# Attention followed by a mixture of experts on one core: how expert weights are loaded, and the last expert's second layer

## The chip, the core and the metric

The kernel runs on one core of a Trainium2 chip, as one program. The time is that of the whole program on the device, in microseconds (us). The core has five engines with a queue each: TensorE (PE, matrix products into the accumulator memory PSUM), VectorE (DVE), ScalarE (ACT), GpSimd (POOL) and SyncE (SP). Here SP issues most of the transfers (DMA), POOL the indirect ones, ACT a few. Each queue is worked off in order, so an instruction that waits holds up everything behind it.

## The reference

```
scores = (q @ k^T) / sqrt(64);  scores = cap * tanh(scores / cap)     # 8 batches x 12 heads, 448 x 448
attn   = softmax(scores);  x = attn @ v, as 3584 tokens x 768
probs  = softmax(x @ w_gate)           # 8 experts; each token goes to its argmax, gate = that probability
for each expert e: the (at most capacity = 80) tokens with the largest gates
    out[token] = gate * (relu(x[token] @ w1[e]) @ w2[e])              # w1: 768 x 1024, w2: 1024 x 768
all other rows of out are zero
```

All data are fp32.

## The kernel before

The attention runs in 24 units (3 of each batch), one per turn of a loop over `w` (line 1488). A turn works through a list of steps (STEPS, at the end LAST, lines 1470 to 1472): `q` score products, `e` exponentials, `v` and `r` products with the values, `x` the place where rows of the PE array change banks (`swap`, line 1221), `l` transfers, `b` background work. The turn `w == NU` has no scores left; its `q` steps begin the first expert (`begin`, line 1450).

Tokens of the first five batches are ranked early, so four experts can be chosen and their tokens fetched before the attention ends. The expert part then runs 84 jobs in a fixed order (line 819): a0, a1, b0, a2, b1, a3, b2, b3, a4, a5, b4, b5, where a is an expert's first layer (6 chunks of weights, 512 KB each) and b its second (8 chunks, 384 KB each). `chunk` (line 859) multiplies one chunk with the tokens in three groups `g` of 32 and four column blocks `j`. After a second layer, `put` (line 892) weights the result with the gates, 12 copies of 32x192 from PSUM to `ys`, and POOL scatters `ys` to the output.

Weights come through a ring of buffers in the order of the jobs: 8 buffers of their own (`wpre`) and 10 (`w3`, line 1545) that lie where the attention's tiles were, 18 in all. `more(n)` (line 826) issues loads on SP until n have been issued. It is called in each turn's transfers (line 1485), for the 8 own buffers, and then once per job (line 1604), always 18 chunks ahead. A load waits until its buffer is free. The transfers on SP and ACT share eight completion counters in turn (DMAHW0 to DMAHW7); a transfer also waits for the one that used its counter before.

The rows of `x` (tile `xb`) of a batch are written to DRAM by four transfers on SP (`write`, line 1277), and the gates of those tokens (tile `gr`) by one more (`send`, line 342), for the last batch on ACT's queue. After both, POOL gathers the tokens of experts 4 and 5 from there (`fetch`, line 1572), ACT and POOL cut them into pieces (`xq`), and DVE turns them into `xt`.

For the last expert (vi = 5, tiles `hp5a`, `hp5b`, `yp5a`, `yp5b`), the second layer's result lies in two PSUM banks: groups 0 and 1 in `yp5a`, group 2 in `yp5b`, and its 12 copies are divided between ACT (even j) and DVE (odd j). `compare` and `decide` (lines 908, 937) set a flag that all engines read at the end (line 1639).

## Time and profile before

| | |
|---|---|
| median of 3 runs | 455.82 us (454.74 to 456.12) |
| the profiled execution | 456.44 us |
| its span on the core | 454.67 us |
| granted TensorE clock, mean | 0.987 of full speed |
| busy share PE, DVE, ACT, POOL | 95%, 51%, 73%, 54% |
| bytes moved | 101.22 MB, 223 GB/s over the span |

The profile is of the one profiled execution. A page gives busy time of each engine and the chain of waits that ended last; the same trace answers for any stretch what an engine did, what ended the idle time before an instruction (in square brackets) and how full the 16 DMA engines were. PE instructions overlap, so the time of a merged row divided by its count is the pace, and PE ends are modelled. The attention fills about the first 345 us, the experts the rest.

### The profile page before, as it was taken

What the parts mean: (1) busy time and instruction counts of PE and PEld (TensorE: products, weight loads), DVE (VectorE), ACT (ScalarE), POOL (GpSimd) and SP (SyncE); (2) the same over time, 40 slices, a digit from 0 to 9 for tenths busy, and PEclk for the clock granted to TensorE, in tenths of its full rate; (3) what the DMA queues carried; (4) which work ended last, traced back from release to release, by engine and by line L of the source; (5) the groups of instructions that cost most, each with busy time, mean ns of one, the idle gap of its engine ahead of it and who ended that gap; (6) DMA issues with size and microseconds to landing.
All of it is one profiled execution on the core that took longest, in us unless ns stands there. A gap on an engine that the chain in (4) does not pass through costs nothing.

```text
span 454.7 us, 21513 instructions
## 1 busy us (share of the span) xinstructions
PE 432.4 (95%) x9533; PEld 230.3 (51%) x9533; DVE 233.8 (51%) x756; ACT 331.4 (73%) x386; POOL 246.4 (54%) x277
## 2 busy tenths in 40 slices
PE   7899999999999999999999999999899999989990
PEld 4344544654444444445444544544346766677680
DVE  1033345337534563776259897977855886210002
ACT  5999989989998988897889988879601154257142
POOL 1767766767765675765576766857655110331000
PEclk9899999999999999999999999999999999999996
DMA  6667695697769559863834862874839997999961
GB/s 158 176 176 203 198 268 160 180 288 211 204 179 269 155 162 276 234 187 99 229 88 133 219 176 82 245 207 147 241 107 360 409 414 275 308 368 410 411 253 38
DMA packets 70549, 101.22 MB, mean 223 GB/s; under 512 B 15264, under 2 KB 52896, under 8 KB 70448
## 3 DMA queue, kind: packets, MB, share of 16 engines
q1 hardware_dynamic: 69072, 96.31, 67.9%
q0 software_dynamic: 752, 3.26, 2.3%
q8 instruction: 77, 1.26, 1.2%
q10 hardware_dynamic: 624, 0.18, 0.2%
q14 instruction: 24, 0.20, 0.1%
HBM read 76.13 MB, written 23.90 MB: 220 GB/s over the span
## 4 chain that ended last, share of the span: by engine, by line
PE 75%; DVE 10%; DMA 7%; ACT 3%; issue 2%; POOL 1%; SPq 1%; POOLq 0%; DVEq 0%; ACTq 0%
PE av L1213 22%; PE sc L1179 22%; PE hp L865 6%; PE yp L865 5%; PE sp L1213 4%; PE av L1246 3%; PE sc L1171 3%; DMA w<-in_w_dram 2%; PE sp L1244 2%; PE lgp L1292 2%; DVE gb L515 2%; DMA xge<-xs,gi 1%; PE pd L447 1%; PE hp5a L865 1%; DMA vr<-in_v_dram 1%
## 5 line engine op out<-in xcount | busy, mean ns | idle before, releaser
L1180 ACT ACTIVATE e<-sc 128x896 f32<-128x896 f32 x168 | 150.9, 913 | 31.1 <-PE sc L1179 28.8
L1213 PE MATMUL av<-e,vr 64*32 64x448 f32 x2304 | 164.5, 538 | 2.0 <-DMA vr<-in_v_dram 1.2
L1179 PE MATMUL sc<-qt,kt 64*32 64x448 f32 x2304 | 143.6, 544 | 3.1 <-ACT e L1180 2.7
L1191 POOL TENSOR_TENSOR t<-e 128x448 f32<-128x448 f32 x92 | 104.7, 1159 | 75.1 <-ACT e L1184 75.1
L1184 ACT ACTIVATE e<-e 128x1792 f32<-128x1792 f32 (+1 forms) x96 | 144.7, 1507 | 0.8
L1194 POOL TENSOR_TENSOR t<-t,e 128x448 f32<-128x448 f32 x92 | 104.5, 1158 | 31.9 <-ACT e L1184 31.9
L1213 PEld LDWEIGHTS av<-e,vr 64*32 64x32 f32 x2304 | 54.4, 107 | 61.6 <-issue 40.6
L1179 PEld LDWEIGHTS sc<-qt,kt 64*32 64x32 f32 x2304 | 42.2, 106 | 47.3 <-issue 32.3
L1254 DVE STREAM_TRANSPOSE st<-sp 128x448 f32<-128x448 f32 x24 | 15.6, 650 | 68.4 <-PE sp L1213 65.2
L1246 PE MATMUL av<-e,vr 64*32 64x224 f32 x384 | 46.6, 349 | 0.0
L1213 PE MATMUL sp<-t,ones 64*32 64x448 f32 x368 | 45.2, 536 | 0.0
L901 POOL DMA_INDIRECT out_dram<-ysv,si x6 | 6.7, 1111 | 69.2 <-ACT ysv L900 62.6
L865 PE MATMUL hp<-w,xt 128*32 128x256 f32 x720 | 41.7, 380 | 1.1 <-DVE xt L693 1.1
L865 PE MATMUL yp<-w,thv 128*32 128x192 f32 x960 | 40.8, 326 | 1.7 <-DMA w<-in_w_dram 1.7
L1246 PE MATMUL av<-e,vx 64*32 64x224 f32 x384 | 42.1, 349 | 0.0
L900 ACT ACTIVATE ysv<-yp,gq 32x192 f32<-32x192 f32 x60 | 24.8, 413 | 16.3 <-PE yp L865 7.9
L865 PEld LDWEIGHTS yp<-w,thv 128*32 128x32 f32 x960 | 32.0, 110 | 9.1 <-issue 2.5
L1266 DVE TENSOR_TENSOR x<-av,r 128x448 f32<-128x448 f32 x48 | 27.7, 618 | 14.4 <-PE av L1213 14.4
L865 PEld LDWEIGHTS hp<-w,xt 128*32 128x32 f32 x720 | 23.5, 110 | 16.3 <-issue 2.3
L1246 PEld LDWEIGHTS av<-e,vr 64*32 64x32 f32 x384 | 22.4, 107 | 16.6 <-issue 15.7
L441 DVE TENSOR_SCALAR_CACHE_REDUCE gb<-krow,kc 112x896 bf16<-112x896 f32 (+7 forms) x36 | 29.8, 871 | 0.6 <-PE pd L447 0.6
L1244 PE MATMUL sp<-e,ones 64*32 64x224 f32 x384 | 28.4, 349 | 0.0
(254 smaller groups left out, 443.0 us busy)
## 6 DMA issues: line engine op xcount, KB each, us to landing
w<-in_w_dram SPq DMA_DIRECT2D x36, 512.0 KB, 8.5
w<-in_w_dram SPq DMA_DIRECT2D x48, 384.0 KB, 8.1
vr<-in_v_dram SPq DMA_DIRECT2D x24, 512.0 KB, 3.9
out_dram<-zero SPq DMA_DIRECT2D x14, 768.0 KB, 5.4
xs<-xb SPq DMA_DIRECT2D x32, 336.0 KB, 6.2
kt<-in_k_dram SPq DMA_DIRECT2D x46, 224.0 KB, 5.4
qt<-in_q_dram SPq DMA_DIRECT2D x46, 224.0 KB, 5.3
vx<-in_v_dram SPq DMA_DIRECT2D x48, 32.0 KB, 3.7
```

The costliest lines, as they stand in the source:

```text
L441: nc.vector.tensor_scalar(g, krow[:, x:y], kp, 0.0, op0=ALU.is_ge, op1=ALU.add, accum_out=a)
L865: nc.tensor.matmul(spot(ps, g, q)[32 * j:32 * j + 32], of(g), w[:, q * j:q * j + q], start=(kk == 0 and g % 2 == 0), stop=(kk == last and ...
L900: nc.scalar.activation(dst, src, AF.Copy, scale=gate(g))
L1179: nc.tensor.matmul(ps[32 * m:32 * m + 32, h, :S], st["k", u][w, pr, y:y + 32], st["q", u][w, pr], start=True, stop=True)
L1180: nc.scalar.activation(st["e", u][:, 2 * x:2 * x + 2], ps[:, :, :S], AF.Tanh, scale=st["regs"][0])
L1184: nc.scalar.activation(e, e, AF.Exp, scale=st["regs"][1])
L1191: nc.gpsimd.tensor_tensor(t1[:, h], e[:, h], e[:, 2 + h], op=ALU.add)
L1194: nc.gpsimd.tensor_tensor(st["es", u, pr][:, h], st["es", u, pr][:, h], e[:, 4 + h], op=ALU.add)
L1213: behind(nc.tensor.matmul(ps[32 * g:32 * g + 32, :S], v_, e, start=first, stop=final))
L1244: behind(nc.tensor.matmul(st["sp", u][32 * g:32 * g + 32, HQ * i:HQ * i + HQ], ones[w, 0:32], e, start=(part == 0), stop=False))
L1246: behind(nc.tensor.matmul(st["av", u, f][32 * g:32 * g + 32, HQ * i:HQ * i + HQ], last_of(u, pr, h, i)[w, 32 * f:32 * f + 32], e, start=Fa ...
L1266: nc.vector.tensor_tensor(st["x", u][:, f], st["av", u, f][:, :S], st["r", u], op=ALU.mult)
```

## The change

- The ring has 21 buffers: 9 of their own, 6 at the low end of the memory that the attention leaves and 6 at its high end, as pools of one buffer each, used in the order 5, 4, 3 of the high ones, the six low ones, 0, 1, 2 of the high ones.
- In each turn's transfers `more` may go one step of its formula further, up to 9.
- In the last turn the marker of `swap` is put on ACT's queue, before on SP's.
- The row writes and the gates' writes are declared independent of each other (`apart_from`).
- In `compare` a memset goes from POOL to DVE.
- The last expert's second layer gets four banks: group 0 in `yp5a`, group 1 in `yp5b`, group 2 in `yp5c` (j = 0, 1) and `yp5d` (j = 2, 3). Its first five chunks run as before, its last three (TAIL) group by group: the three chunks of group 0, then its copies, and so on. DVE copies `yp5a` and `yp5c`, ACT `yp5b` and `yp5d`.

```diff
@@ -45,8 +45,11 @@
 CAPMIN = 1.0e-6
 KD = DM // 128
 KF = F // 128
-WPRE = 8
-WMORE = 10
+WPRE = 9
+WLOW = 6
+WHIGH = (5, 4, 3, None, 0, 1, 2)
+WMORE = WLOW + 6
+TAIL = 3
 DIRECT = (23,)
 PLACE = (2650, 1500, 1500, 1880, 2250, 1880)
 SUMS = (1500, 6200)
@@ -331,6 +334,12 @@
                 nc.vector.tensor_tensor(ohvb, rev[:C].rearrange("p (a e) -> p a e", a=1).broadcast_to(sh), up(cm), op=ALU.is_equal)
         return logits_of, choice, key, lambda: gate_weights(sm, sh, tau if ps is None else None, rd, w2, b, gdst, queue)
 
+    def apart_from(own, others, w):
+
+        for o in st[others]:
+            tc.declare_no_dep(w.ins, o.ins, reason="rows and gates lie apart")
+        st[own].append(w)
+
     def gate_weights(sm, sh, tau, rd, w2, b, gdst, queue):
         if tau is not None:
             nc.vector.scalar_tensor_tensor(w2, tau, 1.0, rd, op0=ALU.subtract, op1=ALU.mult)
@@ -339,7 +348,8 @@
         nc.vector.tensor_scalar(g, g, -1.0, 1e-9, op0=ALU.mult, op1=ALU.add, accum_out=dump[:C])
         g8 = sm.tile([C, NC, PITCH - DM], F32, name=f"gr{b}", tag="gr")
         nc.vector.reciprocal(g8, g.rearrange("p (c a) -> p c a", a=1).broadcast_to([C, NC, PITCH - DM]))
-        send = lambda: queue.dma_start(gdst, g8)
+        def send():
+            apart_from("gates_out", "rows", queue.dma_start(gdst, g8))
         if st.get("gates") is None:
             send()
         else:
@@ -852,18 +862,22 @@
         j, b = divmod(kk, 2)
         return lambda g: x[:, 2 * g + b, 32 * j:32 * j + 32]
 
-    def spot(ps, g, n):
-
-        return ps[g // 2][:, QF * (g % 2):QF * (g % 2) + n] if isinstance(ps, tuple) else ps[:, g // 2, QF * (g % 2):QF * (g % 2) + n]
-
-    def chunk(ps, x, w, kk, last, n):
+    def spot(ps, g, n, j):
+
+        w = slice(32 * j, 32 * j + 32)
+        if isinstance(ps, list):
+            return ps[g + (g == NG - 1 and j >= 2)][w, 0:n]
+        return ps[g // 2][w, QF * (g % 2):QF * (g % 2) + n] if isinstance(ps, tuple) else ps[w, g // 2, QF * (g % 2):QF * (g % 2) + n]
+
+    def chunk(ps, x, w, kk, last, n, groups=range(NG)):
 
         q = n // 4
         of = (rows_of if n == F else turned_rows)(x, kk)
-        for g in range(NG):
+        own = isinstance(ps, list)
+        for g in groups:
             for j in range(4):
-                nc.tensor.matmul(spot(ps, g, q)[32 * j:32 * j + 32], of(g), w[:, q * j:q * j + q],
-                                 start=(kk == 0 and g % 2 == 0), stop=(kk == last and g > 0))
+                nc.tensor.matmul(spot(ps, g, q, j), of(g), w[:, q * j:q * j + q],
+                                 start=(kk == 0 and (own or g % 2 == 0)), stop=(kk == last and (own or g > 0)))
 
     def product(ps, x, ws, n):
         for kk, w in enumerate(ws):
@@ -889,15 +903,19 @@
         nc.scalar.copy(th, hv)
         return th
 
-    def put(fp, yp, gate, si, tag, last=False, others=None):
-        ys = fp.tile([SL, DM], F32, name=f"ys{tag}", tag="ys", bufs=2)
-        for g in range(NG):
-            for j in range(4):
-                dst, src = ys[32 * g:32 * g + 32, QD * j:QD * j + QD], spot(yp, g, QD)[32 * j:32 * j + 32]
-                if last and j % 2:
-                    nc.vector.tensor_scalar(dst, src, gate(g), None, op0=ALU.mult)
-                else:
-                    nc.scalar.activation(dst, src, AF.Copy, scale=gate(g))
+    def weighted(ys, yp, gate, g):
+        for j in range(4):
+            dst, src = ys[32 * g:32 * g + 32, QD * j:QD * j + QD], spot(yp, g, QD, j)
+            if isinstance(yp, list) and (g == 0 or g == NG - 1 and j < 2):
+                nc.vector.tensor_scalar(dst, src, gate(g), None, op0=ALU.mult)
+            else:
+                nc.scalar.activation(dst, src, AF.Copy, scale=gate(g))
+
+    def put(fp, yp, gate, si, tag, ys=None, others=None):
+        if ys is None:
+            ys = fp.tile([SL, DM], F32, name=f"ys{tag}", tag="ys", bufs=2)
+            for g in range(NG):
+                weighted(ys, yp, gate, g)
         w = nc.gpsimd.indirect_dma_start(out=out, out_offset=bass.IndirectOffsetOnAxis(ap=si, axis=0),
                                          in_=ys, in_offset=None, bounds_check=T - 1, oob_is_err=False)
         if others is not None:
@@ -910,7 +928,7 @@
         d = sm.tile([32, NPRE, 3], F32, name="cd", tag="cd")
         nc.vector.tensor_tensor(d, tk, tks, op=ALU.not_equal)
         m = sm.tile([32, 32], F32, name="cm32", tag="cm32")
-        nc.gpsimd.memset(m, 0.0)
+        nc.vector.memset(m, 0.0)
         nc.vector.tensor_reduce(m[:, 0:1], d, axis=AX.XY, op=ALU.max)
         mt = sm.tile([32, 32], F32, name="cmt", tag="cmt")
         nc.vector.transpose(mt, m)
...
@@ -1218,9 +1236,9 @@
                 tc.add_manual_dep(mm.ins, st.pop("turned").ins.name, SYNC, reason="rows of the array change banks")
             st["mm"] = mm
 
-        def swap():
-
-            st["turned"] = nc.sync.nop()
+        def swap(eng):
+
+            st["turned"] = eng.nop()
             tc.add_manual_dep(st["turned"].ins, st["mm"].ins.name, SYNC, reason="rows of the array change banks")
         SYNC = mybir.DependencyInfo(mybir.DependencyClass.Sync, mybir.DependencyReason.DATA)
 
@@ -1276,8 +1294,7 @@
             if j == NP - 1:
                 def write():
                     for i in range(4):
-                        nc.sync.dma_start(xsr[b, i],
-                                          st["xt", b][32 * i:32 * i + 32])
+                        apart_from("rows", "gates_out", nc.sync.dma_start(xsr[b, i], st["xt", b][32 * i:32 * i + 32]))
                 if b == B - 1:
                     write()
                 else:
@@ -1482,7 +1499,7 @@
             while st["gates"]:
                 st["gates"].pop(0)()
             if st.get("ordered"):
-                more(min(WPRE, 3 * (w - NU + 6) // 2 - 1))
+                more(min(WPRE, 3 * (w - NU + 7) // 2 - 1))
 
         st["gates"] = []
         for w in range(NU + 1):
@@ -1516,7 +1533,7 @@
                 elif k_ == 't':
                     total_of(w - 1)
                 elif k_ == 'x' and w:
-                    swap()
+                    swap(nc.scalar if w == NU else nc.sync)
                 elif k_ == 'l':
                     transfers(w)
                 elif k_ == 's' and w:
@@ -1542,14 +1559,15 @@
     st["banks"].append("sp")
     gate(B - 1)
     ft = ExitStack()
-    w3 = ft.enter_context(tc.tile_pool(name="w3", bufs=WMORE, reuse_waits="tile"))
+    wlow = [ft.enter_context(tc.tile_pool(name=f"wl{i}", bufs=1, reuse_waits="tile")) for i in range(WLOW)]
     fr = ft.enter_context(tc.tile_pool(name="fr", bufs=1, reuse_waits="tile"))
     fp = ft.enter_context(tc.tile_pool(name="fp", bufs=2, reuse_waits="tile"))
+    whigh = [ft.enter_context(tc.tile_pool(name=f"wh{i}", bufs=1, reuse_waits="tile")) for i in range(WMORE - WLOW)]
     hs0 = relu(fp, st["hp"], "v0")
     a2s.close()
     pfh = ft.enter_context(tc.tile_pool(name="pfh", bufs=1, space=PSUM))
     pft = ft.enter_context(tc.tile_pool(name="pft", bufs=2, space=PSUM, side="right"))
-    wring.order += [w3] * WMORE
+    wring.order += [p for i in WHIGH for p in (wlow if i is None else [whigh[i]])]
     bg.append((550, lambda: turned(last_u, 0), 1))
     bg.append((550, lambda: turned(last_u, 1), 0))
     xv, fin = {}, {}
@@ -1620,13 +1638,22 @@
         else:
             if kk == 0:
                 yp[vi] = (pft.tile([128, 2, 512], F32, name=f"yp{vi}", tag="ht") if vi < NV - 1 else
-                          (pft.tile([128, 512], F32, name=f"yp{vi}a", tag="ht"), pfh.tile([128, 512], F32, name=f"yp{vi}b", tag="hp")))
+                          [misc(f"yp{vi}a"), misc(f"yp{vi}b"), pft.tile([128, 512], F32, name=f"yp{vi}c", tag="ht"),
+                           pfh.tile([128, 512], F32, name=f"yp{vi}d", tag="hp")])
                 if vi < NPRE:
                     st["there"]("gates")
                 gt[vi] = gate_at(gq, vi) if vi < NPRE else gate_at(gq2, vi - NPRE)
-            chunk(yp[vi], ht[vi], wts[i], kk, KF - 1, DM)
+            ys = None
+            if vi < NV - 1 or kk < KF - TAIL:
+                chunk(yp[vi], ht[vi], wts[i], kk, KF - 1, DM)
+            elif kk == KF - 1:
+                ys = fp.tile([SL, DM], F32, name=f"ysv{vi}", tag="ys", bufs=2)
+                for g in range(NG):
+                    for back in range(TAIL - 1, -1, -1):
+                        chunk(yp[vi], ht[vi], wts[i - back], kk - back, KF - 1, DM, (g,))
+                    weighted(ys, yp[vi], gt[vi], g)
             if kk == KF - 1:
-                put(fp, yp[vi], gt[vi], si0[:, vi:vi + 1] if vi < NPRE else fin["si"][0:SL, vi - NPRE:vi - NPRE + 1], f"v{vi}", vi == NV - 1, stored)
+                put(fp, yp[vi], gt[vi], si0[:, vi:vi + 1] if vi < NPRE else fin["si"][0:SL, vi - NPRE:vi - NPRE + 1], f"v{vi}", ys, stored)
         nxt = next((j for j in jobs[i:] if j[0] == "b" and j[2] == 0 and j[1] not in ht), None)
         if nxt is not None and kk == 1 and jobs.index(nxt) - i in (KD - 1, KF - 1):
             ht[nxt[1]] = turn(fp, pft, hs[nxt[1]], f"v{nxt[1]}")```

Below stands what the change moves at three places. Rows are instructions in queue order: line, operation, output and inputs, shape, and in brackets the engines and transfer counters it waits for.

SP's queue where the last batch's rows are written, before. `w_8` and `w_9` are second-layer chunks of expert b2 (`w_6` is its first), `xb` the rows.

```order
L842 DMA w_8_6598<-in_w_dram 128x768 [waits DMAHW6_49,PE_49]
L1279 DMA xs<-xb_5547 32x14x192 [waits DMAHW7_49,DVE_49]
L1279 DMA xs<-xb_5547 32x14x192 [waits DMAHW0_49]
L1279 DMA xs<-xb_5547 32x14x192 [waits DMAHW1_49]
L1279 DMA xs<-xb_5547 32x14x192 [waits DMAHW2_49]
L842 ISA
L842 DMA w_9_6619<-in_w_dram 128x768 [waits DMAHW3_49,PE_49]
```

The same place after. The gates' transfer on ACT's queue (`xs<-gr`) has the counter DMAHW1 before and DMAHW5 after.

```order
L852 DMA w_10_6619<-in_w_dram 128x768 [waits DMAHW0_49,PE_49]
L852 ISA
L852 DMA w_11_6637<-in_w_dram 128x768 [waits DMAHW1_49,PE_49]
L1297 DMA xs<-xb_5549 32x14x192 [waits DMAHW2_49,DVE_49]
L1297 DMA xs<-xb_5549 32x14x192 [waits DMAHW3_49]
L1297 DMA xs<-xb_5549 32x14x192 [waits DMAHW4_49]
L1297 DMA xs<-xb_5549 32x14x192 [waits DMAHW5_49]
L852 ISA
L852 DMA w_12_6658<-in_w_dram 128x768 [waits DMAHW6_49,PE_49]
```

Three more chunks (`w_9` to `w_11`) now stand ahead of the four row writes, and it is the fourth of them, no longer the third, that waits for the counter of the gates.

PE at the end of the last expert's second layer, before: `w_11` to `w_13` are its last chunks, `yp5a` and `yp5b` the banks.

```order
L865 MATMUL yp5a<-w_11_7425,thv_7508 32x192 [waits DMAHW1_49]
L865 MATMUL yp5a<-w_11_7425,thv_7508 32x192 x7
L865 MATMUL yp5b<-w_11_7425,thv_7508 32x192 x4
L865 MATMUL yp5a<-w_12_7439,thv_7508 32x192 [waits DMAHW2_49]
L865 MATMUL yp5a<-w_12_7439,thv_7508 32x192 x7
L865 MATMUL yp5b<-w_12_7439,thv_7508 32x192 x4
L865 MATMUL yp5a<-w_13_7453,thv_7508 32x192 [waits DMAHW3_49]
L865 MATMUL yp5a<-w_13_7453,thv_7508 32x192 x7
L865 MATMUL yp5b<-w_13_7453,thv_7508 32x192 x4
```

The same chunks after:

```order
L879 MATMUL yp5a<-w_11_7409,thv_7541 32x192 x3
L879 MATMUL yp5a<-w_12_7425,thv_7541 32x192 [waits DMAHW2_49]
L879 MATMUL yp5a<-w_12_7425,thv_7541 32x192 x3
L879 MATMUL yp5a<-w_13_7441,thv_7541 32x192 [waits DMAHW3_49]
L879 MATMUL yp5a<-w_13_7441,thv_7541 32x192 x3
L879 MATMUL yp5b<-w_11_7409,thv_7541 32x192 x4
L879 MATMUL yp5b<-w_12_7425,thv_7541 32x192 x4
L879 MATMUL yp5b<-w_13_7441,thv_7541 32x192 x4
L879 MATMUL yp5c<-w_11_7409,thv_7541 32x192 x2
L879 MATMUL yp5d<-w_11_7409,thv_7541 32x192 x2
```

Each group now gets its three chunks in a row. When group 0 is complete, 24 matmuls are still to come (48 instructions in the trace, where each matmul is two), and 12 when group 1 is; the last four rows of group 2 (`yp5c` and `yp5d` for `w_12` and `w_13`) follow what is shown.

ACT's copies of the last expert (`ysv` from `yp5a` and `yp5b`, `gq` the gates), before:

```order
L900 ACTIVATE ysv_7713<-yp5a,gq_105 32x192 [waits DMASW0_49,PE_49,Activation_49]
L900 ACTIVATE ysv_7713<-yp5a,gq_105 32x192 [waits DVE_49]
L900 ACTIVATE ysv_7713<-yp5a,gq_105 32x192 [waits DVE_49,Pool_49]
L900 ACTIVATE ysv_7713<-yp5a,gq_105 32x192 [waits DVE_49]
L900 ACTIVATE ysv_7713<-yp5b,gq_105 32x192 [waits PE_49]
L900 ACTIVATE ysv_7713<-yp5b,gq_105 32x192 [waits DVE_49]
```

The same after, up to the flag that every engine reads at the end:

```order
L912 ACTIVATE ysv_7712<-yp5b,gq_105 32x192 [waits PE_49,DMASW0_49,Activation_49,Pool_49]
L912 ACTIVATE ysv_7712<-yp5b,gq_105 32x192 x3
L912 ACTIVATE ysv_7712<-yp5d,gq_105 32x192 [waits PE_49]
L912 ACTIVATE ysv_7712<-yp5d,gq_105 32x192
L1666 TENSOR_LOAD fl_i [waits DVE_49]
```

The waits for DVE between ACT's copies are gone; DVE's copies (of `yp5a` and `yp5c`) have none for ACT from the second on.

## Rows read from the trace of the kernel before

**Rows 1.** Busy us by stage: length, PE, PEld, DVE, ACT, POOL, clock, DMA share, GB/s:

```profile
326.00:342.00 16.00, 14.89 (x267) 6.35 (x255) 10.08 (x28) 0.00 (x0) 8.85 (x19) 1.00 0.47 136
342.00:376.00 34.00, 34.00 (x681) 22.65 (x673) 26.72 (x89) 10.11 (x20) 10.57 (x26) 1.00 1.02 403
390.00:400.60 10.60, 10.60 (x234) 7.71 (x226) 2.07 (x14) 1.77 (x3) 1.94 (x2) 1.00 1.01 330
```

**Rows 2.** PE's waits, 320 to 455 us: total us, times, longest:

```profile
PE yp L865 <- DMA w<-in_w_dram: 1.7, 1, 1.7
PE hp L865 <- DVE xt L693: 1.1, 1, 1.1
```

**Rows 3.** SP's waits, 326 to 455 us:

```profile
SPq L1223 <- PE av L1213: 7.9, 2, 5.3
SPq L1279 <- DMA xs<-gr: 7.5, 1, 7.5
SPq L842 <- PE av L1213: 5.8, 1, 5.8
```

**Rows 4.** The chain that ended last, 370 to 455: start, us, what:

```profile
373.07 1.08 DVE xb L1275 x2
...
379.60 5.28 DMA xs<-gr
...
390.79 11.37 DMA w<-in_w_dram
...
402.29 8.01 PE yp L865 x192
```

**Rows 5.** Timeline of the end: start, us, instruction, idle before and releaser:

```profile
435.84 5.10 ACT L900 ACTIVATE ysv<-yp,gq 32x192 f32<-32x192 f32 x12 [5.27 <-PE yp L865]
...
442.32 0.15 DVE L914 TENSOR_REDUCE cm<-cd 32x1 f32<-32x12 f32 x1 [14.78 <-POOL cm L913]
...
443.25 0.62 PE L865 MATMUL yp5b<-w,thv 128*32 128x192 f32 x5
443.62 0.41 ACT L900 ACTIVATE ysv<-yp5a,gq 32x192 f32<-32x192 f32 x1 [2.69 <-issue]
444.07 0.41 DVE L898 TENSOR_SCALAR ysv<-yp5a,gq 32x192 f32<-32x192 f32 x1 [0.79 <-ACT ysv L900]
...
446.81 0.41 ACT L900 ACTIVATE ysv<-yp5b,gq 32x192 f32<-32x192 f32 x1
446.81 0.42 DVE L898 TENSOR_SCALAR ysv<-yp5a,gq 32x192 f32<-32x192 f32 x1 [0.48 <-ACT ysv L900]
...
448.16 0.42 DVE L898 TENSOR_SCALAR ysv<-yp5b,gq 32x192 f32<-32x192 f32 x1 [0.48 <-ACT ysv L900]
448.86 0.93 POOL L901 DMA_INDIRECT out_dram<-ysv,si  x1 [6.57 <-DVE ysv L898]
```

**Rows 6.** Timeline of PE, last six chunks of b2; expert 4's turn:

```profile
394.55 6.06 PE L865 MATMUL yp<-w,thv 128*32 128x192 f32 x144
...
420.79 0.88 PE L888 MATMUL htv<-ctt,hsv 128*128 128x128 f32 x6
```

**Rows 7.** Timeline of POOL and ACT: two gathers, what waits for them:

```profile
334.85 0.98 POOL L797 DMA_INDIRECT xge<-xs,gi  x1 [0.27 <-POOL xq L809]
339.45 0.18 POOL L687 COPY gq<-xge 128x1 f32<-128x1 f32 x1 [3.62 <-DMA xge<-xs,gi]
...
344.32 4.51 POOL L809 COPY xq<-xge 32x192 f32<-32x192 f32 x12 [4.69 <-DVE xt L693]
...
391.59 1.02 POOL L797 DMA_INDIRECT xgv<-xs,gi  x1 [3.01 <-DVE ff L928]
...
400.79 2.15 ACT L809 COPY xq<-xgv 32x192 f32<-32x192 f32 x6 [5.28 <-DMA xgv<-xs,gi]
...
406.63 10.22 ACT L900 ACTIVATE ysv<-yp,gq 32x192 f32<-32x192 f32 x24
418.13 0.81 ACT L876 ACTIVATE hsv<-hp 128x768 f32<-128x768 f32 x1 [1.28 <-PE hp L865]
```

More of the change, by code (lines that the diff above doesn't have):

```diff
@@ L1089, in vector @@
         clock[1] = max(clock[0] + at, clock[1]) + cost
-    st = {"laid": set(), "banks": ["misc"], "held": {}, "take": None, "read": 0, "late": False}
+    st = {"laid": set(), "banks": ["misc"], "held": {}, "take": None, "read": 0, "late": False, "rows": [], "gates_out": []}
     def use(n, f, pe=0):
```

## The prediction, made before the changed kernel ran

> **What bounds the kernel now.** I read the busy shares first: PE 95% over the span, so time can come only from stretches in which PE stands still or has ended. Next the busy time by stage [rows 1]: from 342 us on PE is full, and so are the 16 DMA engines (share 1.02, 403 GB/s), while between 326 and 342 us PE works and the DMA engines stand half empty (0.47). The reader is to see that the experts' weights arrive about as fast as PE uses them: a chunk of a second layer (0.393 MB) takes 0.98 us at 403 GB/s, and PE needs 1.01 us for one (six in 6.06 us, [rows 6]).
>
> Then PE's waits [rows 2]: in the expert part one wait for weights, 1.7 us. The chain of waits [rows 4] shows where it comes from. The gates' transfer is issued at 379.60 and lands at 384.88. SP waited for it with the third of the four row writes in hand (7.5 us, [rows 3]), and all weights stand behind that in SP's queue. Six loads later the chain is at a chunk that is issued at 390.79, lands at 402.16 and lets PE start the second layer of expert 3 at 402.29.
>
> Last the end [rows 5]. PE's last matmuls end at 443.87 (443.25 + 0.62). ACT and DVE then make 12 copies in turn, each waiting 0.48 us and more for the other, from 443.62 to 448.58 (448.16 + 0.42): 4.96 us. Only from 446.81, with ACT in the second bank, do two copies run at once, and only for one pair. POOL's scatter follows, and the span ends at 454.67, 6.09 us after the last copy.
>
> **The change, part by part.**
>
> *Larger ring, earlier loads, marker on ACT.* Between 326 and 342 us SP waits 7.9 us for the two markers of the bank changes and 5.8 us for memory that PE's last value products still read [rows 3], 13.7 us together. Afterwards the markers are on ACT, and the first 10 chunks behind the 8 of before lie in a ninth buffer of their own, in the high part or in the first low part, which is free sooner. Three more chunks, 1.18 MB, are 2.9 us of transfer at 403 GB/s, and fit into those 13.7 us. So SP should come to the row writes no later than before, with three more chunks loaded: through the sixth chunk of b2 where it was the third. Then the first chunk that is missing is b2's seventh. PE wants it at 394.55 + 4 x 1.01 = 398.59 [rows 6].
>
> *Independence of rows and gates.* The order of the instructions shows that the fourth row write waits for the counter that the gates' transfer uses, as the third did. So this edit alone I cost at nothing: SP still stands until 384.88, and goes on with one row write in hand instead of two. The next load is issued by about 385.5. Even with the longest landing on the chain, 11.37 us, it is there at 396.9, 1.7 us before PE wants it. The eighth chunk and the first of b3 follow at 1.19 us each (0.393 MB at the 330 GB/s of 390 to 400.6, [rows 1]), at 398.1 and 399.3, against 399.6 and 400.6. The wait goes: 1.68 us. Its bounds are 0 (the pause eats the lead) and 1.68; more is excluded since the other waits of PE [rows 2] are for engines, not for weights.
>
> *The marker on ACT.* ACT is idle from 326 to 342 us (0.00 busy, [rows 1]), so the marker passes at once, and PE has a chunk of the first expert between marker and next use. Value 0. If ACT were late the price would be what PE waits beyond that chunk; no row shows such a wait, and I bound it by 0 and 1 us.
>
> *Memset on DVE.* Before, DVE's check waited 14.78 us for POOL's memset behind a scatter, until 442.32 [rows 5]. Alone that was free, but group 0's copies stand behind the check in DVE's queue, and they are to start at about 440. The memset itself, some 0.1 us on a DVE that waits anyway, costs nothing; left on POOL it would hold the copies up by about 2 us.
>
> *Four banks, groups in turn.* I place it on the clock of before and take the 1.68 off at the end. 192 instructions of a second layer take 8.01 us [rows 4], so the 24 of one group's last three chunks take 1.00 us: group 0 is complete at 441.87, group 1 at 442.87, group 2 at 443.87. DVE needs 4 copies of some 0.45 us for group 0, to 443.7, and two more to 444.8. ACT is through with expert 4 at 440.94 [rows 5]; its copies take 5.10/12 = 0.425 us each: group 1 from 442.92 to 444.62, two of group 2 to 445.47. ACT ends last, and 448.58 becomes 445.47: 3.1 us. More chunks or fewer in PE's row cost nothing there, since the count of matmuls is the same. Bounds: if the copies still take turns, four of the 12 at least start early, at 441.92, and end 4.96 us later at 446.9, a gain of 1.7; if ACT's share were hidden as DVE's is, both would end near 444.8, a gain of 3.8. A loss is excluded, because no copy starts later than before. I take 3.1, from the rows of the very same copies.
>
> Why the copies took turns decides this term. In the rows, ACT and DVE wait for each other as long as both read `yp5a`, and stop when ACT goes to `yp5b` [rows 5]: one bank, one reader. The Trainium skill (PSUM — Partial Sum Buffer, "PSUM bank collisions raise a hardware error") says that two engines must be kept apart per bank and quadrant of 32 partitions. ACT's even and DVE's odd column blocks lie in different quadrants, so by the page they could have run side by side in the old bank: 6 copies each, to 443.62 + 6 x 0.43 = 446.2, a gain of 2.4 without any new bank. The trace shows waits by bank; it is those that the new banks take away.
>
> **The sum.** 1.68 + 3.1 = 4.8 us off the span: 454.67 becomes 449.9. The profiled execution took 456.44 us, 1.77 more than its span, and the median of the runs, 455.82, is 0.62 below it. So 455.82 - 4.8 = 451.0.
>
> **Rivals.**
>
> *The weights are late anyway* (chance 0.12). SP reaches the row writes with the ring full and must wait there for DVE (`xb`, done at 374.15, [rows 4]) and then for the gates, so the stream may stand from about 371 to 385, longer than before. If the gates land as late as 11.37 us after their issue, at 390.97, the next load lands at about 402.9, 4.3 us after PE wants it, more than is won; if they land 3.4 us later than before, at 388.3, it lands at 400.3 and PE waits about 1.7. For it speaks that a 14 KB transfer took 5.28 us [rows 4]; against it that the DMA engines will have less ahead of it. With the whole gain of the stall gone: 455.82 - 3.1 = 452.7.
>
> *The copies still take turns* (0.06). The waits could come from the shared output tile `ys`. Against it: the pair at 446.81 runs at once and writes the same `ys` [rows 5], and the order of the instructions has lost these waits. Gain 1.7 + 1.68: 452.4.
>
> *Slower: the late gather becomes the bound* (0.03). Experts 4 and 5 need rows gathered at 391.59; ACT begins to cut them at 400.79, then makes 24 copies without a pause until 416.85, and the relu of expert 4 comes 1.28 us after that, waiting for PE [rows 7]. With PE 1.68 us earlier its transposes want to start at 419.11 (420.79 before, [rows 6]); the relu can start at 416.87 and end at 417.68, so 1.43 us of slack are left. Every us beyond that costs PE one. For a time above 457.2 the gather would have to land 1.43 + 4.8 + 1.4 = 7.6 us later than it does, at 408.4, and take 16.8 us instead of 9.2. For it speaks that under the full stream a gather took 9.2 us, and 4.6 when the engines were half empty (334.85 to 339.45, [rows 7]); against it that this stretch was full before too (share 1.01, [rows 1]), and that the row writes which the gather needs come earlier. The Trainium skill (DMA: Bandwidth & Descriptors, "Issuing engines are not separate DMA queues") says that transfers from all queues run on the same 16 engines and interleave; by it the gather at 334.85, which now meets the stream, would also take 9.2 us and land at 344.05. The rows give that no price: POOL went on with those rows only at 344.32, after 4.69 us of waiting for DVE.
>
> **How the numbers follow.** The forecast gets 0.74, the rivals 0.12, 0.06 and 0.03; 0.05 is left for a gain lost among small waits with no change as result. A measurement here can tell about 0.3% (1.4 us) from no change. Faster: 0.74 + 0.12 + 0.06 = 0.92; same 0.05; slower 0.03. The range: below, the upper bound of the tail (0.7 more) and the spread of the runs of before (about 0.7 to each side) give 449.7; above, it takes in both milder rivals, 452.7 with some of that spread: 453.0.
>
> **What would show it.** Right: no PE wait for weights after 342 us; DMA share well above 0.47 between 326 and 342; the fourth row write still waiting for the gates; DVE's group 0 copies beside PE's last matmuls; last copy about 1.6 us after PE's last matmul. Wrong: PE waiting in b2 or b3, ACT and DVE alternating, relu of expert 4 without an idle time before it and PE waiting for its transposes, or anything slower before 342 us.

## The result and the profile after

The changed kernel took 451.23 us (median of 11 runs, 450.33 to 453.97), beside 456.09 us (median of 11, 454.71 to 457.77) for the kernel before, measured with it: a ratio of 0.9891 with a 95% interval of 0.987 to 0.9913. The forecast was 451.0, between 449.7 and 453.0. Two more measurements, on the second and third chip of the experiments below, gave 0.9906 (0.9874 to 0.9938) and 0.9888 (0.9836 to 0.9939). The profiled execution took 452.08 us, with a span of 450.2 and a mean granted clock of 0.993 (before 456.44, 454.67 and 0.987).

PE's waits after 320 us (total, times, longest), against [rows 2]:

```profile
PE av L1231 <- DMA vr<-in_v_dram: 1.2, 1, 1.2
PE pcp L782 <- POOL rh L767: 0.7, 1, 0.7
PE hp L879 <- DVE xt L703: 0.6, 1, 0.6
```

The wait for weights is gone. The stages against [rows 1], columns as there:

```profile
326.00:342.00 16.00, 15.36 (x272) 6.81 (x276) 10.56 (x28) 0.47 (x1) 8.93 (x19) 1.00 1.01 384
...
390.00:400.60 10.60, 10.60 (x240) 7.94 (x234) 2.38 (x16) 3.78 (x9) 3.43 (x8) 1.00 1.02 372
402.40:435.00 32.60, 32.60 (x668) 23.04 (x664) 2.13 (x9) 15.11 (x35) 3.65 (x8) 1.00 0.90 357
```

Between 326 and 342 us the DMA engines are now full (0.47 before), and after 402 they have room (0.90, before 1.03), because the weights are ahead. SP's waits after 320 us, against [rows 3]:

```profile
SPq L852 <- DMA w<-in_w_dram: 23.1, 31, 2.6
...
SPq L852 <- PE hp L879: 12.2, 15, 1.9
SPq L1297 <- DMA xs<-gr: 5.7, 1, 5.7
...
SPq L852 <- PE av L1231: 4.9, 1, 4.9
...
SPq L1241 <- PE av L1231: 1.8, 1, 1.8
```

The markers of the last turn no longer stand in SP's queue (7.9 us before; the 1.8 us shown are for a marker of the turn before, and end at 320.13). SP now waits 12.2 us for PE to free a buffer: the ring is full. It still waits for the gates (5.7 us), with the fourth row write. The end, against [rows 5] (start, us, instruction, idle before and releaser):

```profile
440.48 1.70 DVE L910 TENSOR_SCALAR ysv<-yp5a,gq 32x192 f32<-32x192 f32 x4 [13.13 <-PE yp5a L879]
441.53 1.69 ACT L912 ACTIVATE ysv<-yp5b,gq 32x192 f32<-32x192 f32 x4 [1.82 <-PE yp5b L879]
442.33 0.83 DVE L910 TENSOR_SCALAR ysv<-yp5c,gq 32x192 f32<-32x192 f32 x2 [0.16 <-PE yp5d L879]
443.23 0.84 ACT L912 ACTIVATE ysv<-yp5d,gq 32x192 f32<-32x192 f32 x2
444.35 0.92 POOL L919 DMA_INDIRECT out_dram<-ysv,si  x1 [3.45 <-ACT ysv L912]
```

PE's last matmul ends at 442.30. Groups of copies run back to back, DVE and ACT side by side for most of the time, and the last ends at 444.07, 1.77 us after PE (4.72 before).

Executions differ by up to 3 us in the attention part: PE's first expert matmul starts between 326.4 and 329.6 us in the fourteen profiles. So profiles are compared by three pieces that this shift doesn't touch: from the last 16 matmuls of PE's small product for the late experts (`pcp`, 388.71 in before, 389.01 in after) to PE's end; from there to the last copy; from there to the end of the span.

| kernel | pcp to PE's end | to last copy | to span's end | ratio to before (95%) |
|---|---|---|---|---|
| before | 55.16 | 4.72 | 6.09 | |
| before, again | 54.43 | 4.75 | 6.01 | 1.0009 (0.9989 to 1.003) |
| after | 53.29 | 1.77 | 6.16 | 0.9891 (0.987 to 0.9913) |
| after, again | 53.35 | 1.78 | 6.04 | 0.9906 (0.9874 to 0.9938) |
| after, third | 53.46 | 1.77 | 6.13 | 0.9888 (0.9836 to 0.9939) |
| tail alone | 55.20 | 1.84 | 7.14 | 0.9935 (0.9905 to 0.9965) |
| stream alone | 54.84 | 4.75 | 6.13 | 0.9989 (0.9967 to 1.0012) |
| marker on SP | 55.44 | 1.82 | 6.00 | 0.994 (0.9911 to 0.9968) |
| ring of 18 | 55.80 | 1.83 | 6.07 | 0.9905 (0.987 to 0.994) |
| ring of 18, again | 53.90 | 1.77 | 6.47 | 0.9888 (0.9845 to 0.9931) |
| memset on POOL | 53.01 | 2.33 | 6.53 | 0.9929 (0.9889 to 0.997) |
| one bank each | 55.41 | 3.21 | 6.93 | 0.9992 (0.9962 to 1.0023) |
| six chunks by groups | 53.09 | 0.94 | 6.54 | 0.9876 (0.9851 to 0.99) |
| and two scatters | 53.09 | 0.94 | 5.70 | 0.9884 (0.9861 to 0.9907) |

In the first pair of profiles 1.87 us are gone before PE's end and 2.95 behind it. That the spans differ by 4.44 and not by 4.75 is the 0.3 us by which after came to `pcp` later. The third piece holds POOL's start and the landing of the last scatter. That landing took 3.3 to 3.8 us from POOL's start in the twelve other profiles with one last scatter, but 4.46 in the tail alone: hence its 7.14.

### The profile page after: what moved, and what is told of

Its sections match the earlier page's. It is cut to its first block, busy times and chain, and to the rows that moved or that the text cites. A ratio compares the mean times of both kernels' runs of the same rounds, so it can differ in the third digit from the quotient of the medians.

```text
span 450.2 us, 21504 instructions
## 1 busy us (share of the span) xinstructions
PE 432.3 (96%) x9533; PEld 227.6 (51%) x9533; DVE 233.9 (52%) x757; ACT 331.2 (74%) x386; POOL 245.9 (55%) x276
## 4 chain that ended last, share of the span: by engine, by line
PE 85%; DVE 6%; DMA 3%; ACT 2%; POOL 1%; issue 1%; SPq 0%; POOLq 0%; DVEq 0%
PE av L1231 23%; PE sc L1197 23%; PE yp L879 9%; PE hp L879 8%; PE sp L1231 4%; PE sc L1189 3%; PE av L1264 3%; PE sp L1262 2%; PE lgp L1309 2%; PE pd L457 1%; ACT e L1198 1%; PE hp5a L879 1%; DMA xge<-xs,gi 1%; ACT e L1202 1%; DMA w<-in_w_dram 1%
## 5 line engine op out<-in xcount | busy, mean ns | idle before, releaser
L1231 PE MATMUL av<-e,vr 64*32 64x448 f32 x2304 | 165.9, 540 | 2.0 <-DMA vr<-in_v_dram 1.2
L1197 PE MATMUL sc<-qt,kt 64*32 64x448 f32 x2304 | 145.1, 546 | 4.1 <-ACT e L1198 3.8
L1231 PEld LDWEIGHTS av<-e,vr 64*32 64x32 f32 x2304 | 54.4, 107 | 61.6 <-issue 41.5
L1231 PE MATMUL sp<-t,ones 64*32 64x448 f32 x368 | 45.5, 536 | 0.0
L919 POOL DMA_INDIRECT out_dram<-ysv,si x6 | 6.7, 1109 | 67.2 <-ACT ysv L912 67.2
L879 PE MATMUL hp<-w,xt 128*32 128x256 f32 x720 | 42.2, 380 | 0.6 <-DVE xt L703 0.6
L879 PE MATMUL yp<-w,thv 128*32 128x192 f32 x960 | 40.7, 327 | 0.0
L912 ACT ACTIVATE ysv<-yp,gq 32x192 f32<-32x192 f32 x60 | 24.8, 412 | 16.3 <-PE yp L879 7.9
L879 PEld LDWEIGHTS yp<-w,thv 128*32 128x32 f32 x960 | 31.3, 110 | 8.1 <-issue 0.3
L879 PEld LDWEIGHTS hp<-w,xt 128*32 128x32 f32 x720 | 23.1, 110 | 16.8 <-issue 2.7
```

The lines of the kernel that those rows point to most:

```text
L879: nc.tensor.matmul(spot(ps, g, q, j), of(g), w[:, q * j:q * j + q], start=(kk == 0 and (own or g % 2 == 0)), stop=(kk == last and (own or ...
L912: nc.scalar.activation(dst, src, AF.Copy, scale=gate(g))
L1197: nc.tensor.matmul(ps[32 * m:32 * m + 32, h, :S], st["k", u][w, pr, y:y + 32], st["q", u][w, pr], start=True, stop=True)
L1231: behind(nc.tensor.matmul(ps[32 * g:32 * g + 32, :S], v_, e, start=first, stop=final))
```

## The experiments

The first four ran on one chip.

**Tail alone** (before, with the new end of the last expert and nothing else).

In short:

```
-    yp = (pft.tile([128, 512]), pfh.tile([128, 512]))
+    yp = [misc, misc, pft.tile([128, 512]), pfh.tile([128, 512])]
+    last 3 chunks: for g in groups: the 3 chunks of g, then weighted(g)
-    nc.gpsimd.memset(m, 0.0)
+    nc.vector.memset(m, 0.0)
```

> The kernel before, with the last expert's part of the change alone (four banks, the last three chunks by groups, DVE for group 0 and half of group 2, the memset on DVE); ring, marker and row writes as before. Theory (the two gains are separate and add): PE's one wait of 1.7 us for weights at about 400 us stays, PE's last matmul ends where it did before, and from there to the last copy it takes 1.8 us where it took 4.71: 2.9 us faster than before, about 453.1. Rival (the tail only pays because PE ends earlier, or the copies of group 0 are held by something else in the old stream): less than 1.5 us faster, above 454.6.

Measured: 453.71 us, ratio 0.9935, 3.0 us of 457.19. The last copy is 1.84 us after PE's end. The tail's part stands on its own. But in this execution PE had no wait for weights, though the stream was that of before. It stood still at three places, 2.1 us together counted from the starts of its matmuls, and the profile gives no releaser for it: it calls such idle time "issue", time in which the engine waited for nothing that the profile shows. The weights would have been in time without it too: b3's first chunk landed 2.07 us before PE began on it, and 1.46 of the 2.1 us lie ahead of that place.

**Stream alone** (after with the end of before: the reverse of the diff above).

> The kernel after with the old end (two banks, all chunks by turns, DVE and ACT in alternate columns, memset on POOL): only ring, marker and row writes are changed against before. Theory: no wait of PE for weights after 342 us, PE's last matmul 1.6 us earlier than before, and 4.7 us from there to the last copy as before: 1.6 to 1.7 us faster than before, about 454.4. Rival (the stall's end is given back at expert 4 or 5, where ACT cuts the late gather): PE's last matmul less than 0.8 us earlier, 455.3 or more.

Measured: 456.88 us, ratio 0.9989, 0.5 us and not to be told from none. With the 3.0 us of the tail alone that makes 3.5 on this chip, not the 4.8 of the sum. The wait for weights is gone as expected, yet PE's part is 54.84 us, since PE stood still elsewhere (start, us, instruction, idle before):

```profile
392.24 1.11 PE L875 MATMUL yp<-w,thv 128*32 128x192 f32 x17
393.72 1.55 PE L875 MATMUL yp<-w,thv 128*32 128x192 f32 x31 [0.37 <-issue]
...
396.01 10.27 PE L875 MATMUL yp<-w,thv 128*32 128x192 f32 x244
406.57 3.93 PE L875 MATMUL yp<-w,thv 128*32 128x192 f32 x90 [0.29 <-issue]
```

Both breaks lie inside a chunk, where no matmul waits for anything. Their full cost is read from the starts: 48 matmuls that take 2.07 us in before (391.68 to 393.75) took 2.96 here (392.24 to 395.20). The rival named another place (expert 4's late gather) and isn't what happened.

**Marker on SP.**

```
-    swap(nc.scalar if w == NU else nc.sync)
+    swap(nc.sync)
```

> The kernel after with the markers of the last window's bank changes back on SP's queue. Theory (the three chunks more that lie ahead of the row writes are what took PE's wait away, and SP has time for them even when it stands 7.9 us for the markers, since the 5.8 us for memory are gone): SP waits some 8 us between 326 and 342 again, the DMA share there falls from 1.01 to 0.6 to 0.8, PE has no wait for weights, and the time is that of after within 0.5 us. Rival (SP must not stand at the markers): the sixth chunk of b2 is not issued before the row writes or lands late, PE waits 0.8 to 1.7 us for weights, 452 to 453.

Measured: 454.34 us, ratio 0.994. SP waits 7.6 us for the two markers of the last turn, the DMA share from 326 to 342 is 0.67, and no wait for weights appears: as expected. The standstills can hardly have hidden one: counted from `pcp`, the load that PE waited for in before was issued 4.1 us earlier than there, and the standstills ahead of it come to 1.0 us. The time isn't as expected: PE stands still by the name of issue again, 2.3 us together, 1.2 of them at one place (start, us, instruction, idle before):

```profile
396.45 10.29 PE L879 MATMUL yp<-w,thv 128*32 128x192 f32 x244
407.64 3.93 PE L879 MATMUL yp<-w,thv 128*32 128x192 f32 x90 [0.90 <-issue]
```

**A ring of 18.** In short:

```
-WPRE = 9; WHIGH = (5, 4, 3, None, 0, 1, 2); WMORE = WLOW + 6
+WPRE = 8; WHIGH = (3, None, 0, 1, 2); WMORE = WLOW + 4
-    more(min(WPRE, 3 * (w - NU + 7) // 2 - 1))
+    more(min(WPRE, 3 * (w - NU + 6) // 2 - 1))
```

> The kernel after with a ring of 18 buffers (8 and 10, as before) where it has 21; markers on ACT and the new end as in after. Theory of the prediction (the lead of three chunks takes the wait away, the pause for the gates stays): b2's fourth chunk is the first behind the row writes again, PE waits 0.8 to 1.7 us for weights, 452.0 to 452.9. Rival (the gates land sooner, 2.7 us after their issue where before took 5.28, since the DMA engines have worked off the weights by then, and the stream resumes 1.8 us earlier): with a full ring of 18 the engines are as quiet, loads resume near 383 us, PE waits 0.3 us at most, and the time is that of after.

Measured: 453.38 us, ratio 0.9905; no wait for weights, but 2.5 us of the other standstills, which could have hidden one. Undecided, so it ran again below. The next four ran on a second chip.

**Before and after again.**

> The kernel before once more, with a second profile. Three of the four runs so far that should have lost PE's wait for weights show other standstills of PE in the second layers of experts 1 to 3, put down to issue, 1.3 to 2.2 us together, at the 8756th and the 8884th matmul record, 128 matmuls apart, each ending 2.3 to 2.5 us after the start of a 16 KB packet of the instruction queue. Theory A (such a standstill is made of an instruction load that starts too late for PE, it comes and goes between executions, and before has it too, in place of or beside the 1.7 us for weights): PE waits 1.5 to 3 us in the expert part, by one name or the other, and the end is as in the first profile, 4.7 us from PE's last matmul to the last copy. Theory B (only the changed streams have it): one wait of 1.7 us for weights and no other.

> The kernel after once more, with a second profile, beside the runs of one chip with the variants. Theory A (instruction loads come late in some executions): a standstill of PE of up to 1.3 us at the 8756th matmul record if the 16 KB load before it starts when fewer than 2.4 us of matmuls are left, and then a span of 451.5 to 452.5 against 450.2 in the first profile; ratio to before 0.989 to 0.994. Theory B (only the variants have it): no standstill there, ratio 0.989.

Measured: before 456.06, after 451.07 us, ratio 0.9906. Before waits 0.9 us for weights at the same place (1.68 in its first profile), 0.1 for those of expert 5's second chunk, and 0.2 by issue at expert 4's first; after has no standstill but 0.2 to 0.3 us. So neither theory holds as it stands: A asked for 1.5 to 3 us in before, and against B the streams of before and after are not free of standstills everywhere (see the last group).

**Six chunks by groups.**

```
-TAIL = 3
+TAIL = 6
```

> The kernel after with the last six chunks of the last expert by groups in place of three. Theory (the first two groups are complete 4 and 2 us before PE's end, so all their copies are done by then, and after PE's last matmul only two copies on DVE and two on ACT are left): last copy 0.9 us after PE's end instead of 1.77, 0.85 us faster than after. Rival (PE starts the groups later or stalls, since it reads six chunks in turn; or the copies after PE's end still wait): PE's end later by over 0.3 us, or last copy over 1.4 us after it, and the same time as after.

**And two scatters.** In short:

```
-    scatter(out, si, ys)
+    scatter(out, si[0:64], ys[0:64]); scatter(out, sl, ys[64:96])
```

> As the kernel with the last six chunks by groups, and the last expert's scatter in two: the first 64 rows as soon as groups 0 and 1 are copied, the last 32 rows alone at the end (three small DVE operations more for their indices). Theory (the 6.1 us from the last copy to the end of the span depend on how many rows the last scatter writes): 0.3 to 1 us off these 6.1 us. Rival (they are a fixed cost of the scatter on POOL and of its landing, and the first scatter stands ahead of the second on POOL): 6.1 us or more.

Measured: 451.1 and 450.7 us, ratios 0.9876 and 0.9884. The last copy is 0.94 us after PE's end in both, as forecast. Of these 0.83 us the first kernel gives half back. Its end (columns as above):

```profile
443.34 0.83 DVE L910 TENSOR_SCALAR ysv<-yp5c,gq 32x192 f32<-32x192 f32 x2 [2.11 <-PE yp5d L879]
443.40 0.84 ACT L912 ACTIVATE ysv<-yp5d,gq 32x192 f32<-32x192 f32 x2
444.97 0.92 POOL L919 DMA_INDIRECT out_dram<-ysv,si  x1 [3.05 <-ACT ysv L912]
```

The end of the kernel with two scatters:

```profile
441.02 0.83 DVE L910 TENSOR_SCALAR ysv<-yp5c,gq 32x192 f32<-32x192 f32 x2 [2.11 <-PE yp5d L879]
441.08 0.84 ACT L912 ACTIVATE ysv<-yp5d,gq 32x192 f32<-32x192 f32 x2
441.22 0.92 POOL L921 DMA_INDIRECT out_dram<-ysv,si  x1 [1.61 <-ACT ysv L912]
442.67 0.89 POOL L921 DMA_INDIRECT out_dram<-ysv,sl  x1 [0.53 <-issue]
```

POOL starts the scatter 0.73 us after the last copy, in after 0.28. POOL waits for DVE in an instruction of its own and for ACT in the scatter; in after DVE ends 0.9 us before ACT, so the first wait is long over, here both end together. The small last scatter lands 2.4 us after its start (442.67 to 445.04), the whole one in after 3.5 (444.35 to 447.83); this rests on one profile. From `pcp` to the end of the span the last kernel takes 59.7 us, after on the same chip 61.2, before 65.2 to 66.0: 1.4 us better than after by these pieces, which the runs' ratios can't tell apart.

The last four ran on a third chip.

> The kernel after a third time, beside the ring of 18 on the same chip. From PE's small product for the late experts (pcp, the first of its last 16) to PE's end it took 53.3 us in both profiles so far, and 54.8 to 55.8 us in the four variants of the first chip, with 1.3 to 2.2 us of standstills put down to issue. Theory A (the standstills belong to a chip, or to an execution on it): this run has them wherever the ring of 18 has them, and not where that has none. Theory B (they belong to the variants): 53.3 us here, 55 us and more in the ring of 18.

> The kernel after with a ring of 18 a second time. Its first profile had no wait for weights, but 2 us of other standstills, which could have hidden one. Theory of the prediction (three chunks of lead are what takes the wait away): where the other standstills are absent, PE waits 0.8 to 1.7 us for weights and the time is 0.8 to 1.7 us above after's on the same chip. Rival (the stream resumes earlier after the gates, 384.5 us against 386.0 in before, and that is enough for 18 buffers): no wait for weights, the time of after within 0.5 us.

Measured: after 451.83 us (0.9888), the ring of 18 451.66 (0.9888). After has standstills of 0.1 and 0.2 us, the ring of 18 of 0.6 and 0.2, at two of the places of the first chip but smaller, and no wait for weights. So the rival holds: with the rest of the change in place, 18 buffers are enough. In the trace b3's first chunk, the one PE waited for in before, lands 0.1 us before PE starts on it in both profiles of before, 4.6 us before in the ring of 18 and 11.2 in after. When SP resumes the weights shows why. SP's timeline in before (start, us to the end of the last one, instruction, count):

```profile
375.98 9.76 SPq L1279 DMA_DIRECT2D xs<-xb  x4
385.98 12.41 SPq L842 DMA_DIRECT2D w<-in_w_dram  x13
```

The same in the ring of 18:

```profile
373.66 8.72 SPq L1297 DMA_DIRECT2D xs<-xb  x4
382.62 4.15 SPq L852 DMA_DIRECT2D w<-in_w_dram  x7
```

In after, with 21 buffers and the marker on ACT too:

```profile
374.50 8.41 SPq L1297 DMA_DIRECT2D xs<-xb  x4
383.15 0.37 SPq L852 DMA_DIRECT2D w<-in_w_dram  x1
```

And with 21 buffers and the marker on SP:

```profile
376.12 9.85 SPq L1297 DMA_DIRECT2D xs<-xb  x4
386.21 0.37 SPq L852 DMA_DIRECT2D w<-in_w_dram  x1
```

Counted from the end of `xb` (374.15, 373.63, 374.47, 375.19), SP resumes after 11.8, 9.0, 8.7 and 11.0 us. All fourteen profiles divide in this way: 11.0 to 12.1 us in the five with the marker on SP (before twice, tail alone, one bank each, marker on SP), 8.7 to 9.3 in the nine with it on ACT, whether the ring has 18 buffers or 21. With the marker on ACT the loads ahead of the row writes are all issued before the rows are ready, so three row writes start at once (374.50 in after). And when the gates' transfer is issued, no weights are under way: in after the last of them landed at 376.86, the gates were issued at 379.92 and took 2.7 us. In before the last weights landed at 382.53, the gates were issued at 379.60 and took 5.28.

**Memset on POOL.**

```
-    nc.vector.memset(m, 0.0)
+    nc.gpsimd.memset(m, 0.0)
```

> The kernel after with the memset of the check back on POOL. Theory (POOL gets to it only behind the scatter of expert 4, 0.95 us after that begins, and DVE's group 0 copies stand behind the check in its queue): DVE starts them 1.4 us later than in after, 0.3 us before PE's end in place of 1.8, and ends its six copies 2.2 us after PE's end; the last copy is then DVE's, 0.4 to 0.5 us later than in after. Rival (the check has slack enough, or ACT's copies end last anyway): the last copy 1.8 us after PE's end as in after.

Measured: 453.68 us, ratio 0.9929. DVE's group 0 copies start 0.2 us before PE's end (1.8 in after), the last copy is DVE's, 2.33 us after PE's end, and POOL follows after 0.80 instead of 0.28 us: 1.1 us in all by the trace, twice what was expected. The ratio can't be told from that of after on the same chip (0.9888, 0.9836 to 0.9939). The timeline of its end:

```profile
439.85 0.11 POOL L931 MEMSET cm<- 32x32 f32 x1
440.00 0.15 DVE L932 TENSOR_REDUCE cm<-cd 32x1 f32<-32x12 f32 x1 [14.78 <-POOL cm L931]
...
440.99 1.70 DVE L910 TENSOR_SCALAR ysv<-yp5a,gq 32x192 f32<-32x192 f32 x4
442.14 0.84 ACT L912 ACTIVATE ysv<-yp5d,gq 32x192 f32<-32x192 f32 x2
442.70 0.84 DVE L910 TENSOR_SCALAR ysv<-yp5c,gq 32x192 f32<-32x192 f32 x2
444.34 0.93 POOL L919 DMA_INDIRECT out_dram<-ysv,si  x1 [4.37 <-DVE ysv L910]
```

**One bank for each engine** (before with one line changed).

```
-    if last and j % 2:
+    if last and g < 2:
```

> The kernel before with one word changed: at its end DVE takes the eight copies of groups 0 and 1, which lie in one bank, and ACT the four of group 2, in the other (before: every second column block to DVE, in both banks). Theory (ACT and DVE take turns because they read one bank): no waits of one for the other, DVE's eight copies back to back, the last copy 8 x 0.43 = 3.4 to 3.6 us after PE's end in place of 4.7, 1.2 us faster than before. Rival (they take turns for another reason, the shared output tile): the copies go on waiting for each other, 4.7 us or more.

Measured: 455.79 us, ratio 0.9992. The copies no longer wait for each other, and the last ends 3.21 us after PE (4.72):

```profile
443.46 3.41 DVE L898 TENSOR_SCALAR ysv<-yp5a,gq 32x192 f32<-32x192 f32 x8
443.87 1.69 ACT L900 ACTIVATE ysv<-yp5b,gq 32x192 f32<-32x192 f32 x4 [2.79 <-PE yp5b L865]
447.67 0.93 POOL L901 DMA_INDIRECT out_dram<-ysv,si  x1 [5.25 <-ACTq L1640]
```

So the turns came from the shared bank, not from the shared tile. Of the 1.5 us won 0.5 go to POOL's later start (it waits for two engines here) and 0.3 to a slower landing of the scatter (3.73 us, 3.41 in before). PE stood 1.9 us by the name of issue in this execution, with before's stream, and the ratio can't show the rest.

## Why the prediction was right, and where not

*The whole.* 4.8 us were forecast and 4.86 measured (456.09 to 451.23). The tail's share is shown by runs of its own. That of the weight stream is read from traces; alone it gave 0.5 us, with PE's other standstills in its place, so that the sum comes out as well as it does is in part luck.

*Four banks and groups: 3.1 us forecast, 2.95 measured.* Every step holds: groups complete in turn, copies of 0.42 us, ACT last. The difference is the start of ACT's last two copies, 0.93 us after PE's end where a gapless row gave 0.75. The tail alone and the bank experiment confirm it. The Trainium skill's rule by quadrant (PSUM — Partial Sum Buffer, "PSUM bank collisions raise a hardware error") would have had ACT and DVE side by side in one bank; the waits that this kernel carries go by bank in every run, and whether the chip needs them was not tried.

*The wait for weights: 1.68 forecast, 1.87 measured up to PE's end.* Here the result was right and the reason only in part. That the two numbers lie so near is luck too: by the starts of its matmuls the wait cost before 1.87 us, before lost 0.3 more in its last chunks, and after lost 0.4 at about 410.5 where before lost nothing. In the second pair of profiles the wait is 0.9 us, and PE's part differs by 1.08.

The step that failed is "SP still stands until 384.88": SP went on at 383.15, 8.7 us after `xb` instead of 11.8, since the gates took 2.7 us and not 5.28, and one row write stood behind them instead of two. The first rival had this point ("the DMA engines will have less ahead of it"), the sum didn't. And "Value 0" for the marker on ACT looked only at ACT and PE; SP's time was booked as room for three more loads. By the runs the marker is worth 2.3 of these 3.1 us (11.0 to 8.7, with 21 buffers in both). The three chunks more, which the sum made the cause, are not needed once the marker is on ACT (ring of 18), and the marker isn't when they are there (marker on SP): with the rest of the change in place, either removes the wait. The marker alone in the kernel before, and the new places of the buffers in memory, were not tried by themselves. A second profile of before showed the wait at 0.9 us, and two executions with its stream had 0.3 and none, so its worth varies from 0 to 1.7 us.

*Memset: about 2 us of delay if left on POOL.* The delay of the copies is 1.6 us, its price 1.1.

*Independence of rows and gates: nothing.* Taken out of the changed kernel, it leaves every instruction and every wait on all engines as it is; so it has no effect here.

*Rivals.* The weights were not late: SP did stand before the row writes with all loads issued, but the next load (b2's seventh chunk) was issued at 383.15 and landed at 387.22. The copies no longer take turns; they did so for the bank and not for `ys`, as one bank for each engine shows. The slower case is dead: the late gather took 7.8 us, 9.2 before, and expert 4's relu came after 2.58 us of waiting for PE (1.28 before). The early gather, which now meets the full stream, took 7.05 us (335.16 to 342.21), between the two rows of before (4.6 beside half-empty engines, 9.2 under the full stream). POOL's next copies still waited 2.25 us more for DVE, so it cost nothing. The Trainium skill (DMA: Bandwidth & Descriptors, "Issuing engines are not separate DMA queues") has transfers of all queues run on the same 16 engines and interleave; this trace agrees, 7.05 us against 4.6, at less than the full price of 9.2.

*What the forecast didn't see* is PE's standstill by the name of issue. Counted by the starts of matmuls against six chunks by groups, the row with the least of it but one, it comes to 0.2 to 0.4 us in the three profiles of after, and to 1.7 to 2.7 us in the four variants on the first chip, as much as the wait that was removed or more.

## What to carry to other kernels

Where two engines drain one accumulator, give each a bank of its own and let the matmuls finish them in turn; and see which engine the last consumer waits for last. A marker in the queue that issues loads can cost more than its own wait: the loads that it delays are still under way when the small transfer behind them is issued, and the next shared counter hands that on (here 2.3 us more of pause). When a stall is removed on an engine that runs full, look for what comes next on the same engine before the whole gain is booked.

## What was not expected of the hardware

Instructions are loaded by DMA too. The profile lists 16 KB packets of the kind "instruction" on queue q8, one about every 6.1 to 6.5 us under the full stream. The two breaks, at the 8756th and the 8884th matmul record, are 128 apart, so by estimate a packet holds some 128 matmuls with their weight loads; in second layers PE needs 128 matmuls in 5.2 us (192 in 7.80, 402.29 to 410.09 in before). In six profiles (those of the four variants of the first chip, the ring of 18 again, one bank each) PE goes on 2.3 to 2.6 us after the start of such a packet.

How far ahead the packet starts goes with the standstill in all fourteen profiles. At record 8756 it is 0.14 us or less where the packet starts 55 matmuls ahead or more (nine profiles, after among them with 63), 0.6 with 43 and 47, and 1.2 to 1.35 with 27 to 30. At record 8884 it is nothing with 47 or more (before, twice), 0.1 to 0.2 with 43, 0.4 with 35 to 39, and 0.7 to 0.8 with 31 to 34. This fits an instruction load that comes too late for PE. That it is one was argued from these times, not tried: no run moved a packet on purpose. What stays open: the other break, 6 to 27 records before the 8500th, seen in the four variants of the first chip alone, and whether chip, execution or stream decides when a packet starts.
